# Sixteen rows of an output-weight load moved from SyncE to GpSimd, in pieces of 8191 elements and 1

## The chip, the cores and the metric

The kernel runs on one core of a Trainium2 chip. The metric is the device time of one execution in microseconds. Three runs of the kernel before gave 387.35, 387.57 and 392.26 us; their median is 387.57. The profiled execution took 387.31 us, of which 385.3 lie between the first and the last instruction.

## What is computed

A block for one decoded token in a batch of four: an adaptive layer norm, attention over a cache of 4096 positions with 32 query heads on 8 key/value heads, an output projection, a second adaptive layer norm, and a small mixer network. All is float32.

```
mod = (silu(c) @ w_mod).reshape(4, 6, 1, 512); sa, ca, ga, sb, cb, gb = mod[:, 0..5]
h = layernorm(x) * (1 + ca) + sa
q = (h @ wq), 32 heads of 128; k, v from the caches (4, 8, 4096, 128), each used by 4 query heads
o = softmax(q k^T / sqrt(128)) v
x = x + ga * (o @ wo)                       # wo is (32*128, 512)
h = layernorm(x) * (1 + cb) + sb
x = x + gb * (gelu(h * w1 + b1) @ w2 + b2)  # h is (4, 512), w1 and w2 have 1792 values
```

## The kernel before, in words

Nearly all bytes are the caches: 32 pairs of batch row and key/value head (index `i`, batch row `i // 8`, head `i % 8`), each with 2 MB of keys and 2 MB of values. With the query weights (8 MB), the output weights (8 MB) and the modulation weights (6 MB) the kernel reads 157.3 MB.

SyncE (SP) issues all loads. Its queue holds them in program order: the first modulation weights `wm01`, the small weights `sm` (two DMAs, rows 0 to 15 and rows 16 to 127, lines 50 and 51), `x`, two query-weight tiles, the keys of pairs 0 and 1 (`load_first`), and then one 4 MB tile per step that holds the keys of pair `i + 2` beside the values of pair `i` (`load_pair`, line 165). These 4 MB tiles, the query weights and some modulation weights share a ring of three buffers (`ring`, tag `kv`). So SP waits before an issue until TensorE has done with the buffer, and the DMA engines have two or so loads queued ahead meanwhile. The output weights have buffers of their own: `wo_p` (line 84) is four tiles of two heads each, 128 partitions by 4096 elements, and `load_wo` (line 171) loads one of them. They are loaded at lines 570 and 579 to 580: heads 0 and 1 before the loop, heads 2 and 3 in step 1, heads 4 and 5 in step 3, heads 6 and 7 in step 5.

Per pair, `scores` (line 217) multiplies the query with the keys into PSUM, VectorE reduces the row maximum, TensorE turns and spreads it, ScalarE takes the exponential, VectorE transposes the result in blocks, `values` (line 281) multiplies it with the values, and two steps later `project` (line 327) multiplies the head's output with that head's output weights `wo_t[h]`. A loop (lines 577 to 617) does pairs 0 to 23; the last eight follow an order written by hand (`PLAN`, line 626), in which the loads get shorter towards the end, the last ones being pieces of the values of pair 31 and then 1 MB of modulation weights. `Mixer` does the second half of the block for the first three batch rows between the attention steps; the last batch row's is the tail (`finish`, line 528).

GpSimd does small operations: constants, a few elementwise operations at the start up to the copy into `rows` (line 141), and then only the inverse square roots `root` (line 90) and `wr` (line 421) of the mixers.

Of the kernel before, what the change touches and what calls it, by code (L numbers as in the profile page):

```python
# [8 lines left out]
F32 = mybir.dt.float32  # L9
# [5 lines left out]
B, D, HQ, HKV, SK, DH, F = 4, 512, 32, 8, 4096, 128, 1792  # L15
REP = HQ // HKV
NF = F // 128
EPS = 1e-5
P = 128
NS = B * HKV  # L20
NSM = 3 * NF + 16 + 1


WIDE = {NS - 5: 24, NS - 4: 32}
NARROW = NS - 3


@with_exitstack
def adaln_decode(ctx: ExitStack, tc: tile.TileContext, small, x, wmod, wq, kk, kv, vv, wo, out):
    nc = tc.nc  # L30
    pad = ctx.enter_context(tc.tile_pool(name="pad", bufs=1))
    ring = ctx.enter_context(tc.tile_pool(name="ring", bufs=3))
    wos = ctx.enter_context(tc.tile_pool(name="wos", bufs=1))
# [12 lines left out]
    sm = cst.tile([P, NSM], F32, name="sm")  # L46
    xr = wk.tile([P, D], F32, name="xr", tag="yw", bufs=1)[0:B]
    wm01 = ring.tile([P, 2, 4, D], F32, name="wm01", tag="kv")
    nc.sync.dma_start(wm01, wmod[0])
    for lo, hi in ((0, 16), (16, P)):  # L50
        nc.sync.dma_start(sm[lo:hi], small[lo:hi])
    nc.sync.dma_start(xr, x)
    wqt = []
    for k in range(0, 4, 2):
# [26 lines left out]
    nc.gpsimd.memset(QT, 0.0)  # L81
    hT = cst.tile([P, 4, 32], F32, name="hT")
    nc.gpsimd.memset(hT, 0.0)
    wo_p = [wos.tile([P, 2, REP, D], F32, name=f"wo{h}") for h in range(0, HKV, 2)]
    wo_t = [wo_p[h // 2][:, h % 2] for h in range(HKV)]
    prep = cst.tile([P, 4, P], F32, name="prep")
    osb = cst.tile([P, B, P], F32, name="osb")
# [77 lines left out]
    def load_pair(i):  # L165
        t = slots()
        nc.sync.dma_start(t, kv[i])
        key(t[:, 0], i + 2)
        value(t[:, 1], i)

    def load_wo(h):
        nc.sync.dma_start(wo_p[h // 2], wo[h // 2])

    def load_wm24():
        w = ring.tile([P, 3, 4, D], F32, name="wm24", tag="kv")
# [133 lines left out]
    def pick(i):  # L309
        po = PV.pop(i)  # L310
        n, m = po.shape[-1] // DH, WIDE.get(i, 1)
        if i in OT:
# [255 lines left out]
    load_first()  # L568
    load_pair(0)
    load_wo(0)  # L570
    for i in range(2):
        for step in (scores, row_max, turn_max, col_max, spread_max, copy_max, expo):
            step(i)
# [3 lines left out]
    for i in range(NS - HKV):  # L577
        load_pair(i + 1)
        if i in (1, 3, 5):
            load_wo(i + 1)  # L580
# [155 lines left out]
```

## Time and profile before

| | us |
|---|---|
| median of three runs | 387.57 |
| profiled execution | 387.31 |
| its span, first to last instruction | 385.3 |
| TensorE busy in the span | 295.1 |
| VectorE busy | 195.9 |
| ScalarE busy | 111.5 |
| GpSimd busy | 8.5 |
| share of 16 DMA engines' span taken by SP's queue, q1 | 95.2% |

A core has 16 DMA engines. A load is cut into packets, each done by one engine; when an engine has done its part of a load it writes a completion, a packet of 4 bytes. The page gives packets by queue: q1 is SP's, q10 ScalarE's, and q8 and q14 fetch instructions. For a window of the trace the same table counts the packets that start in it, their bytes, and the time that they took as a share of 16 engines' time; from one kind of packet in a short window its duration follows.

### The profile page before, as it was taken

What the parts mean: (1) busy time and instruction counts of PE and PEld (TensorE: products, weight loads), DVE (VectorE), ACT (ScalarE), POOL (GpSimd) and SP (SyncE); (2) the same over time, 40 slices, a digit from 0 to 9 for tenths busy, and PEclk for the clock granted to TensorE, in tenths of its full rate; (3) what the DMA queues carried; (4) which work ended last, traced back from release to release, by engine and by line L of the source; (5) the groups of instructions that cost most, each with busy time, mean ns of one, the idle gap of its engine ahead of it and who ended that gap; (6) DMA issues with size and microseconds to landing.
All of it is one profiled execution on the core that took longest, in us unless ns stands there. A gap on an engine that the chain in (4) does not pass through costs nothing.

```text
span 385.3 us, 5577 instructions
## 1 busy us (share of the span) xinstructions
PE 295.1 (77%) x2376; PEld 118.0 (31%) x2376; DVE 195.9 (51%) x386; ACT 111.5 (29%) x141; POOL 8.5 (2%) x30
## 2 busy tenths in 40 slices
PE   0777594965856828799987869887788897889984
PEld 0122121311222302244432324342222453433753
DVE  0120441620443504546776544758665566878756
ACT  0001120121110111101577210124574105557266
POOL 1200000000000000000000000000000000000000
PEclk9969756985996979958999995999999999999999
DMA  8999999999999999999999999999999999999920
GB/s 331 432 435 435 413 456 435 405 454 429 412 441 432 427 432 435 430 435 434 432 435 435 430 433 434 432 430 432 427 435 432 430 432 428 422 428 427 416 92 3
DMA packets 7424, 157.68 MB, mean 409 GB/s; under 512 B 980, under 2 KB 1252, under 8 KB 1512
## 3 DMA queue, kind: packets, MB, share of 16 engines
q1 hardware_dynamic: 7392, 157.33, 95.2%
q8 instruction: 18, 0.29, 0.3%
q14 instruction: 6, 0.05, 0.0%
q10 hardware_dynamic: 8, 0.00, 0.0%
HBM read 157.32 MB, written 0.01 MB: 408 GB/s over the span
## 4 chain that ended last, share of the span: by engine, by line
DMA 55%; PE 32%; DVE 7%; ACT 3%; issue 1%; POOL 1%; SPq 0%; POOLq 0%; ACTq 0%; DVEq 0%
DMA kv<-in_kv 53%; PE s L222 8%; PE pv L282 8%; DVE p L258 3%; PE qs L129 3%; DVE m L227 3%; PE s L114 2%; PE pt L319 2%; DMA sm<-in_small 2%; PE pa L333 2%; PE pb L242 1%; ACT uu L538 1%; PE pve L294 1%; PE py L437 1%; PE pm L231 1%
## 5 line engine op out<-in xcount | busy, mean ns | idle before, releaser
L222 PE MATMUL s<-kv,QT 128*32 128x512 f32 x512 | 73.9, 697 | 44.1 <-DMA kv<-in_kv 42.9
L227 DVE TENSOR_REDUCE m<-s 128x1 f32<-128x1024 f32 x32 | 39.2, 1224 | 100.0 <-PE s L222 99.9
L252 ACT ACTIVATE p<-s,nm 128x1024 f32<-128x1024 f32 x32 | 35.6, 1114 | 181.9 <-DVE nm L247 181.8
L282 PE MATMUL pv<-kv,p 128*32 128x512 f32 x464 | 68.2, 655 | 0.5 <-DMA kv<-in_kv 0.5
L222 PEld LDWEIGHTS s<-kv,QT 128*32 128x32 f32 x512 | 15.8, 119 | 87.3 <-DMA kv<-in_kv 56.6
L319 PEld LDWEIGHTS pt<-g,po 128*128 128x128 f32 x236 | 30.6, 202 | 27.8 <-issue 21.3
L333 PE MATMUL pa<-wo,oT 128*32 128x512 f32 x240 | 33.7, 633 | 4.4 <-DVE oT L325 4.2
L319 PE MATMUL pt<-g,po 128*128 128x4 f32 (+2 forms) x236 | 33.4, 265 | 0.9 <-DVE po L305 0.8
L258 DVE STREAM_TRANSPOSE p<-p 128x1024 f32<-128x1024 f32 x25 | 30.9, 1235 | 0.0
L305 DVE COPY po<-pv 128x512 f32<-128x512 f32 x29 | 20.0, 689 | 15.2 <-PE pv L282 15.1
L236 DVE TENSOR_REDUCE mx<-pm 1x128 f32<-1x512 f32 x32 | 21.3, 669 | 1.0 <-PE pm L231 1.0
L426 DVE TENSOR_SCALAR u<-hb,wr,sm 128x512 f32<-128x512 f32 x40 | 19.9, 540 | 1.9 <-POOL wr L421 1.0
L482 ACT ACTIVATE u<-u 128x1024 f32<-128x1024 f32 x20 | 20.4, 1051 | 1.5 <-DVE u L426 1.4
L252 ACT ACT_TABLE_LOAD x11 | 14.1, 1283 | 19.4 <-DVE nm L247 19.3
L349 DVE TENSOR_TENSOR acc<-acc,pa 128x512 f32<-128x512 f32 x26 | 17.8, 686 | 2.8 <-PE pa L333 2.8
L242 PEld LDWEIGHTS pb<-neg,mx 1*128 1x128 f32 x64 | 10.2, 198 | 27.7 <-DVE mx L236 26.0
L114 PE MATMUL s<-wm,sT 128*4 128x512 f32 x16 | 9.2, 744 | 11.7 <-DVE sT L100 11.7
L482 ACT ACT_TABLE_LOAD x13 | 16.7, 1283 | 0.2
L282 PEld LDWEIGHTS pv<-kv,p 128*32 128x32 f32 x464 | 13.6, 146 | 6.8 <-issue 2.8
L231 PE MATMUL pm<-ident,m 128*1 128x128 f32 x32 | 9.1, 283 | 7.6 <-DVE m L227 3.5
L437 PE MATMUL py<-u,sm 128*32 128x512 f32 x80 | 14.5, 593 | 0.0
L242 PE MATMUL pb<-neg,mx 1*128 1x1 f32 x64 | 12.9, 268 | 2.1 <-DVE mx L236 2.1
(134 smaller groups left out, 213.5 us busy)
## 6 DMA issues: line engine op xcount, KB each, us to landing
kv<-in_kv SPq DMA_DIRECT2D x28, 4096.0 KB, 21.7
wq<-in_wq SPq DMA_DIRECT2D x2, 4096.0 KB, 15.8
wo<-in_wo SPq DMA_DIRECT2D x4, 2048.0 KB
kv<-in_kv SPq DMA_DIRECT2D x4, 2048.0 KB, 21.2
wm<-in_wmod SPq DMA_DIRECT2D x2, 2048.0 KB, 24.6
kv<-in_kk SPq DMA_DIRECT2D x1, 4096.0 KB
kv<-in_vv SPq DMA_DIRECT2D x3, 1024.0 KB
wm<-in_wmod SPq DMA_DIRECT2D x1, 1024.0 KB
```

The costliest lines, as they stand in the source:

```text
L222: mm(s[32 * c:32 * c + 32, n * 512:(n + 1) * 512], QT[:, b, h, :], KT[i][:, (n * 4 + c) * 512:(n * 4 + c + 1) * 512], start=True, stop=True)
L227: dv.tensor_reduce(M[i], S[i], axis=AX.X, op=OP.max)
L236: dv.tensor_reduce(mx, M[i].rearrange("o (c r) -> o r c", c=4).unsqueeze(1).to_broadcast([1, 4, 32, 4]), axis=AX.X, op=OP.max)
L242: mm(pb, M[i].rearrange("o c r -> o (c r)"), neg1, start=True, stop=True)
L252: nc.scalar.activation(p, S[i], AF.Exp, bias=M.pop(i), accum_out=l)
L258: dv.transpose(PL[i][0], PL[i][0])
L282: mm(PV[i][32 * q:32 * q + 32, :], pT[:, 128 * k:128 * k + 128:4], VT[i][:, 4 * k:4 * k + 4, :].rearrange("p j d -> p (j d)"), start=(k < ...
L305: dv.tensor_copy(PV[i], pv)
L319: mm(pt, po[:, c * DH:(c + 1) * DH], sel.unsqueeze(1).to_broadcast([P, m, REP]), start=(c == 0), stop=(c == n - 1))
L333: mm(pa[32 * g:32 * g + 32, :], oT[:, g:g + 1].to_broadcast([P, 32]), wo_t[h][:, g, :], start=True, stop=True)
L426: dv.tensor_scalar(u[:, e, :], hb, wr[:, j:j + 1], b1[:, j:j + 1], op0=OP.mult, op1=OP.add)
L482: nc.scalar.activation(u, u, AF.Gelu_apprx_tanh)
```

## The change

The output weights of heads 2 to 5 become one tile `wob` and one array in memory, laid out so that a partition's four heads, 8192 elements or 32 KB, lie in one piece. SP loads rows 0 to 111 of it in two DMAs (two heads each), where and when it loaded all 128 rows before. Rows 112 to 127 are loaded by GpSimd: for each row one DMA of 8191 elements and one of the last element, 32 in all. Heads 0, 1, 6 and 7 are loaded as before. The small weights are loaded in one DMA of 128 rows. The bytes are the same.

```diff
-    for lo, hi in ((0, 16), (16, P)):
-        nc.sync.dma_start(sm[lo:hi], small[lo:hi])
+    nc.sync.dma_start(sm, small)
...
-    wo_p = [wos.tile([P, 2, REP, D], F32, name=f"wo{h}") for h in range(0, HKV, 2)]
+    wo_b = wos.tile([P, 2, 2, REP, D], F32, name="wob")
+    wo_p = [wos.tile([P, 2, REP, D], F32, name=f"wo{h}") for h in (0, HKV - 2)]
+    wo_p[1:1] = [wo_b[:, 0], wo_b[:, 1]]
...
     def load_wo(h):
-        nc.sync.dma_start(wo_p[h // 2], wo[h // 2])
+        if h in (0, HKV - 2):
+            nc.sync.dma_start(wo_p[h // 2], wo[h // (HKV - 2)])
+        else:
+            nc.sync.dma_start(wo_p[h // 2][:LONG], wb[:LONG, h // 2 - 1])
+
+    def load_long():
+        n = 2 * SK
+        flat, src = wo_b.rearrange("p e h g n -> p (e h g n)"), wb.rearrange("p e h g n -> p (e h g n)")
+        for r in range(LONG, P):
+            for lo, hi in ((0, n - 1), (n - 1, n)):
+                nc.gpsimd.dma_start(flat[r:r + 1, lo:hi], src[r:r + 1, lo:hi])
...
     load_wo(0)
+    load_long()
```

`LONG` is 112. In the order of instructions it looks as follows. GpSimd before, around the copy into `rows`:

```order
L101 COPY sT_127<-sT 128x128 [waits DVE_49]
L109 TENSOR_SCALAR ve_139<-mv_137 4x1 [waits DVE_49]
L92 TENSOR_TENSOR yp<-ve_139,half 4x1 [waits Pool_49]
L141 COPY rows<-ident 4x32
L92 TENSOR_TENSOR ye<-mv,half 128x1 [waits DVE_49] x2
```

GpSimd now, from the same copy on (DMASW0 to 7 are eight semaphores that its DMAs use in turn):

```order
L143 COPY rows<-ident 4x32
L184 DMA wob<-in_wb 1x8191
L184 DMA wob<-in_wb 1x1
...
L184 DMA wob<-in_wb 1x8191 [waits DMASW0_49]
L184 DMA wob<-in_wb 1x1 [waits DMASW1_49]
...
L184 DMA wob<-in_wb 1x1 [waits DMASW7_49]
L94 TENSOR_TENSOR ye<-mv,half 128x1 [waits DVE_49] x2
```

The 32 issues stand between the copy and the first inverse square root of the mixers; from the ninth on each waits until the DMA eight places ahead has completed. SP before, from the loads ahead of the loop on (`wo_122` is heads 2 and 3):

```order
L172 DMA wo_121<-in_wo 128x4096
L167 DMA kv<-in_kv 128x8192 [waits DMAHW5_49,DMAHW1_49,PE_49]
L167 DMA kv<-in_kv 128x8192 [waits DMAHW6_49,DMAHW2_49,PE_49]
L172 DMA wo_122<-in_wo 128x4096 [waits DMAHW3_49]
L176 DMA wm_317<-in_wmod 128x4096 [waits DMAHW7_49,PE_49]
```

And now:

```order
L175 DMA wo_121<-in_wo 128x4096
L169 DMA kv<-in_kv 128x8192 [waits DMAHW4_49,PE_49]
L169 DMA kv<-in_kv 128x8192 [waits DMAHW5_49,DMAHW1_49,PE_49]
L177 DMA wob<-in_wb 112x4096 [waits DMAHW2_49]
L188 DMA wm_347<-in_wmod 128x4096 [waits DMAHW6_49,PE_49]
```

The load keeps its place and has 112 rows; SP's semaphores are one number lower, since one DMA less stands ahead of them. TensorE before, at the projection of head 2:

```order
L266 MATMUL pl<-g_115,l 128x4
L333 MATMUL pa<-wo_122,oT 32x512 [waits DMAHW3_49,DVE_49]
L333 MATMUL pa<-wo_122,oT 32x512 x3
L231 MATMUL pm<-ident,m 1x128 [waits DVE_49]
L282 MATMUL pv<-kv,p 32x512 x4
```

And now:

```order
L278 MATMUL pl<-g_114,l 128x4
L345 MATMUL pa<-wob,oT 32x512 [waits DMASW4_49,DMASW6_49,DMASW2_49,DMAHW2_49,DMASW0_49,DVE_49]
L345 MATMUL pa<-wob,oT 32x512 x3
L243 MATMUL pm<-ident,m 1x128 [waits DVE_49]
L294 MATMUL pv<-kv,p 32x512 x4
```

The projection of head 2 waits for GpSimd's long pieces beside SP's load; the order of TensorE's work is the same. In the same way the last matmul of head 5's projection waits for the pieces of one element.

More of the change, by code (lines that the diff above doesn't have):

```diff
@@ L21 @@
 NSM = 3 * NF + 16 + 1
+LONG = 112
 WIDE = {NS - 5: 24, NS - 4: 32}
@@ L28, in adaln_decode @@
 @with_exitstack
-def adaln_decode(ctx: ExitStack, tc: tile.TileContext, small, x, wmod, wq, kk, kv, vv, wo, out):
+def adaln_decode(ctx: ExitStack, tc: tile.TileContext, small, x, wmod, wq, kk, kv, vv, wo, wb, out):
     nc = tc.nc
@@ L717 @@
     v = a["A_v_cache"].reshape(NS, P, SK * DH // P)
+    w = a["A_wo"].reshape(HKV // 2, 2, REP, DH, D)
     arrays = {
@@ L725 @@
         "vv": con(v[NS - 2:]),
-        "wo": con(a["A_wo"].reshape(HKV // 2, 2, REP, DH, D).transpose(0, 3, 1, 2, 4)),
+        "wo": con(w[::3].transpose(0, 3, 1, 2, 4)),
+        "wb": con(w[1:3].transpose(3, 0, 1, 2, 4)),
     }
```

## The prediction, made before the result was known

> **What bounds the kernel now.** I read the page's shares and its chain first, then stretches of the span, then the DMA packets of short windows. From the page: the span, what the 16 DMA engines moved, the queues, and the chain's shares by engine.
>
> ```profile
> span 385.3 us, 5577 instructions
> GB/s 331 432 435 435 413 456 435 405 454 429 412 441 432 427 432 435 430 435 434 432 435 435 430 433 434 432 430 432 427 435 432 430 432 428 422 428 427 416 92 3
> ...
> q1 hardware_dynamic: 7392, 157.33, 95.2%
> q8 instruction: 18, 0.29, 0.3%
> q14 instruction: 6, 0.05, 0.0%
> ...
> DMA 55%; PE 32%; DVE 7%; ACT 3%; issue 1%; POOL 1%; SPq 0%; POOLq 0%; ACTq 0%; DVEq 0%
> ```
>
> From the second slice on the engines move about 432 GB/s until the last two slices. A table of four stretches says the same beside the compute engines (its last two columns are the DMA engines' busy share and GB/s):
>
> ```profile
> core 0: us, PE busy (x) PEld busy (x) DVE busy (x) ACT busy (x) POOL busy (x), PEclk, DMA share, GB/s
> 0.00:20.00 20.00, 8.32 (x15) 1.53 (x16) 1.56 (x5) 1.50 (x2) 3.82 (x19) 1.00 0.94 389
> 20.00:343.00 323.00, 251.52 (x1795) 95.59 (x1792) 164.19 (x309) 87.95 (x113) 3.95 (x9) 0.88 1.00 431
> 343.00:367.00 24.00, 23.39 (x348) 13.04 (x348) 18.95 (x42) 10.75 (x14) 0.00 (x0) 1.00 1.00 420
> 367.00:386.00 19.00, 11.91 (x228) 7.82 (x220) 11.24 (x31) 11.29 (x14) 0.76 (x2) 0.97 0.07 30
> ```
>
> From 20 to 367 us the DMA engines are busy all the time. TensorE has 71 us to spare up to 343, then 0.61 us in the stretch to 367, then 19 us of tail follow. So the end is the end of the stream plus the tail. A load has landed when its slowest engine is done, so what counts is the latest of 16 engines. A completion is a 4-byte packet, one from each engine that a load used; they are the packets under 512 B in these windows. First the end of the load that lands near 18 us, then that of the load near 342 us, cut in three:
>
> ```profile
> DMA packets 32, 0.52 MB, mean 477 GB/s; under 512 B 16, under 2 KB 16, under 8 KB 16
> ```
> ```profile
> DMA packets 59, 0.82 MB, mean 431 GB/s; under 512 B 9, under 2 KB 9, under 8 KB 9
> ```
> ```profile
> DMA packets 21, 0.34 MB, mean 430 GB/s; under 512 B 0, under 2 KB 0, under 8 KB 0
> ```
> ```profile
> DMA packets 26, 0.31 MB, mean 445 GB/s; under 512 B 7, under 2 KB 7, under 8 KB 7
> ```
>
> The first window is 17.1 to 18.2: all 16 engines finish within 1.1 us. The others are 339.2 to 341.1, to 341.9 and to 342.6: nine engines finish in the first 1.9 us, none in the next 0.8, seven in the last 0.7. So seven engines run about 3 us behind the first, and they set the pace. What else those engines carry is the instruction fetches of q8 and q14, 24 packets. One of them, in the window 98.4 to 99.4:
>
> ```profile
> q1 hardware_dynamic: 14, 0.46, 109.6%
> q8 instruction: 1, 0.02, 5.5%
> ```
>
> 5.5% of 16 engines in 1.0 us is 0.88 us of one engine.
>
> **Prices of a packet.** Windows with packets of one size: 20 to 26 us (32 KB), 4.8 to 6.8 (16 KB), and 7.264 to 7.270 (one completion):
>
> ```profile
> q1 hardware_dynamic: 77, 2.52, 97.3%
> ```
> ```profile
> q1 hardware_dynamic: 50, 0.82, 95.5%
> ```
> ```profile
> q1 hardware_dynamic: 1, 0.00, 9.4%
> ```
>
> 0.973 x 16 x 6.0 / 77 = 1.21 us for 32 KB; 0.955 x 16 x 2.0 / 50 = 0.61 us for 16 KB; 0.094 x 16 x 6 ns = 9 ns for a completion.
>
> **The change, part by part.** *Two loads of 112 rows.* How rows go to engines is seen where the small loads end, 7.25 to 8.4:
>
> ```profile
> DMA packets 201, 0.58 MB, mean 504 GB/s; under 512 B 180, under 2 KB 180, under 8 KB 184
> ```
>
> 180 packets are the 128 rows of the small weights and 52 completions; 52 = 16 (modulation weights) + 16 (the 16 rows) + 16 (the 112 rows) + 4 (x, whose 4 rows are the four 2 KB packets). So 112 rows go to 16 engines, seven each, and an engine loses one 16 KB packet in each of two loads: 2 x 0.61 = -1.22 us on every engine. That is the lower end. The upper end is not shown, since the 112 small rows are too short to tell; the packets of such a load could be held up by each other (second rival). I take -1.22, which the nearest row, the 112-row load with seven rows an engine, gives.
>
> *Sixteen long pieces.* 8191 elements are 32764 B, by the rows of 32 KB above one packet of 1.21 us, together 16 x 1.21 = 19.4 us of engine time. Spread evenly this is +1.21 an engine, and nothing is gained or lost. An engine that is missed has 0, one that gets two 2.43; all on one engine would be 19.4 (a rival). The 32 pieces alternate long and short, so if engines are taken in turn, every second engine gets two long ones and the others none. I take 2.43 for the latest engine: with half of the engines drawn, one of the seven late ones is almost surely among them. Net +1.21.
>
> *Completions.* 32 more DMAs: at least one completion each, at most one on all 16 engines, 0.0 to 32 x 9 ns = 0.3 us on an engine. I take 0.1, since x had one for each engine that it used. If each held its engine as the fetch above did (0.88 us against 0.61 for its 16 KB on q1, 0.27 too much), 32 x 0.27 = 8.6 us: the upper end, which I do not take, as a completion carries 4 bytes. The Trainium skill, DMA: Bandwidth & Descriptors, "Why a DMA increments its semaphore by 16 and not by 1", says that a DMA issued by GpSimd completes on all 16 engines whatever its shape, and that one with no common divisor goes to a single engine that a cursor picks in turn; no run here shows either. By it the sum would be 0.2 higher, and there would be no pile on one engine (third rival).
>
> *Small weights in one load.* SP issues one DMA less, and 16 completions go, 9 ns on each engine. SP has nothing to do then until 20.94, and no engine of the stream waits for it:
>
> ```profile
> 1.18 0.87 SPq L51 DMA_DIRECT2D sm<-in_small  x2
> ...
> 20.94 0.33 SPq L161 DMA_DIRECT2D kv<-in_kk  x1
> ```
>
> The weights land at most 0.1 us earlier, and what hides it is the full stream. I count 0; if the cover were gone it would be a gain of 0.1.
>
> *GpSimd's queue and the new wait.* 32 issues stand between two of its instructions, and TensorE's projection of head 2 now waits for them:
>
> ```profile
> 13.32 0.20 POOL L141 COPY rows<-ident 4x32 f32<-4x32 f32 x1
> 173.56 0.57 POOL L92 TENSOR_TENSOR ye<-mv,half 128x1 f32<-128x1 f32 x1 [160.05 <-DVE mv L383]
> ```
> ```profile
> 99.61 1.06 PE L333 MATMUL pa<-wo,oT 128*32 128x512 f32 x8 [0.21 <-DVE oT L325]
> ```
>
> GpSimd is idle for 160 us after its copy, and the pieces have 99.6 - 13.5 = 86 us. Eight are in flight at a time; at SP's 0.44 us an issue the 32 take 14 us, at the 21.7 us in which a large load of SP lands (the page's row below) four rounds take 87. Only then does TensorE stall, by about 1 us, with everything behind the projection, and it has those 71 us to make it up. I count 0.
>
> ```profile
> kv<-in_kv SPq DMA_DIRECT2D x28, 4096.0 KB, 21.7
> ```
>
> *How it reaches the end.* TensorE is idle for 0.61 us between 343 and 367, and what it waited for from the loads between 326 and 368 is
>
> ```profile
> PE s L222 <- DMA kv<-in_kv: 2.4, 3, 1.2
> ```
>
> A later stream moves all that follows by as much; an earlier one is worth at most these 2.4 us.
>
> **Sum.** -1.22 + 2.43 + 0.1 = +1.3 us. The profiled execution took 387.31 us (385.3 of span and 2.0 around it), 0.3 below the median of 387.57. 387.3 + 1.3 = 388.6; against the median 388.9. I say 388.8.
>
> **Rivals.** *Not slower: the late engines are spared.* If the long pieces fall just on engines that are ahead, the seven late ones keep only the -1.22. For: the nine early ones have 0.8 us and more in hand, and the alternation of long and short looks as if it picked engines. Against: a set of every second engine has to miss all seven. The early ones then come 1.2 later, to about 0.3 us before the old end, so 0.3 to 1.1 us are won: 386.2 to 387.0. It decides where no late engine gets two pieces.
>
> *Slower: rows that go to other engines than usual hold each other up.* In loads of 128 rows each engine moves eight rows of its own, undisturbed, at 27 GB/s. If writes to the same rows of SBUF share one engine's rate, then seven rows an engine, shifted against the usual eight, meet the packets of neighbours that are in another load. Each of 14 packets then goes at half speed, +14 x 0.61 = 8.6 us, and each engine is also met by as many, up to 8.6 more; the long pieces add 1.2 (met once) to 4.9 (rows 112 to 127 are four engines' rows, four pieces each). With the -1.2: +7.4 to +20.9, or 395 to 408, middle 402. For: no load of the stream has another shape than 128 rows, so no row excludes it. Against: the packets of the 112 small rows show no stretch. It decides if more than about half of the packets meet another. The Trainium skill speaks for it: SBUF — State Buffer, "Door 1: The DMA port swizzle", gives each group of eight partitions one port with about one engine's rate; that 16 engines of 27 GB/s make 432 here agrees with it, but with a limit of the engines as well.
>
> *Slower: piled up or surcharged.* All long pieces on one engine, as x's four rows went to four engines and a one-row load might always go to the first: 19.4 - 1.2 = 18.2, less up to 3 us if that engine is ahead: 402 to 405. Or 32 completions on every engine at 0.27: 396.
>
> **Chances.** The forecast (387.8 to 390.6) 0.34; late engines spared 0.18; rows that meet 0.32; piled up or surcharged 0.10; rows that meet only now and then (391 to 395) 0.04; more than 2% faster 0.02. 2% is 7.8 us, about what a measurement of this kernel can tell from no change: below 379.8 is faster, above 395.3 slower. Within: 0.34 + 0.18 + 0.04 = 0.56; slower 0.32 + 0.10 = 0.42; faster 0.02. The range leaves out the best of the spared case and the worst third of the meeting one: 386.0 to 404.0. The forecast's own range is 387.8 to 390.6.
>
> **What would show it.** Right: 32 KB packets stay at 1.21 us in all windows, the late completions of the load near 342 us come 1 us later, and the loads land as before up to there. Spared: the seven late completions come earlier. Meeting rows: packets of 16 or 32 KB far over 0.61 and 1.21 us between 14 and 115 us, GB/s under 400 in slices of that part, and all later loads late by the same. Surcharge: the same between 14 and 60 us, with 512 and not 32 new completions. Wrong in any case: a wait of TensorE at the projection of head 2 that costs the end.

## The result and the profile after

The changed kernel takes 432.09 us (median of four runs, 431.37 to 432.37); beside it on the same chip the kernel before took 387.46. The ratio is 1.1145 (95% interval 1.1111 to 1.1179), 44.6 us more. The prediction said 388.8 and at most 404. The profiled execution has a span of 430.1 us; before it was 385.3. Executions that were disturbed are left out of the ratios here and below, so a ratio can differ a little from the quotient of two medians.

These are the page's lines of the changed kernel that answer to those shown of before: the span, GB/s in 40 slices of now 10.75 us, the queues (q0 is GpSimd's), and the chain's shares.

```profile
span 430.1 us, 5614 instructions
...
GB/s 345 427 418 421 414 422 341 255 142 34 360 422 253 388 407 443 282 424 364 421 416 399 420 436 434 433 431 436 343 439 428 419 427 434 431 422 433 409 89 3
...
q1 hardware_dynamic: 7344, 156.81, 89.4%
q0 software_dynamic: 1024, 0.53, 0.6%
...
DMA 54%; PE 28%; another core or an unknown queue 7%; DVE 6%; ACT 2%; issue 1%; POOL 1%; SPq 0%; POOLq 0%; DVEq 0%; ACTq 0%
```

The stream falls to 34 GB/s in the tenth slice (97 to 107 us) and dips again later. The table of stretches of the changed kernel gives its size (the last three columns are the granted TensorE clock, the DMA engines' busy share and GB/s); the stretch from 388 on is the one that before began at 343.

```profile
core 0: us, PE busy (x) PEld busy (x) DVE busy (x) ACT busy (x) POOL busy (x), PEclk, DMA share, GB/s
0.00:20.00 20.00, 8.74 (x16) 1.49 (x16) 1.56 (x5) 1.50 (x2) 8.13 (x27) 1.00 0.93 379
20.00:64.00 44.00, 20.55 (x129) 6.53 (x132) 7.67 (x12) 4.07 (x10) 7.22 (x14) 0.75 1.01 421
64.00:108.00 44.00, 18.58 (x98) 5.84 (x94) 8.34 (x14) 2.41 (x4) 5.24 (x11) 0.59 0.65 193
108.00:150.00 42.00, 23.89 (x158) 6.66 (x154) 9.75 (x18) 4.76 (x9) 0.00 (x0) 0.69 0.99 358
150.00:388.00 238.00, 192.45 (x1420) 76.31 (x1412) 138.60 (x266) 76.39 (x90) 3.95 (x9) 0.92 0.97 413
388.00:412.00 24.00, 23.42 (x346) 13.03 (x348) 18.67 (x42) 11.17 (x14) 0.00 (x0) 1.00 0.95 397
```

And the same stretches of the kernel before, up to 150 us:

```profile
0.00:20.00 20.00, 8.32 (x15) 1.53 (x16) 1.56 (x5) 1.50 (x2) 3.82 (x19) 1.00 0.94 389
20.00:64.00 44.00, 28.64 (x172) 9.01 (x173) 11.52 (x18) 5.27 (x12) 0.00 (x0) 0.73 1.00 431
64.00:108.00 44.00, 33.70 (x237) 10.97 (x233) 15.99 (x28) 5.96 (x11) 0.00 (x0) 0.81 1.00 428
108.00:150.00 42.00, 25.19 (x176) 8.37 (x168) 15.66 (x28) 3.61 (x6) 0.00 (x0) 0.84 1.01 436
```

In bytes: by 150 us the changed kernel has moved 379 x 20 + 421 x 44 + 193 x 44 + 358 x 42 = 49.6 MB, the kernel before 63.9 MB in the same way. The missing 14.3 MB are 33 us at 431 GB/s. From 150 to 388 it moves 413 and not 431: 238 x 18 = 4.3 MB, another 10 us. Those 43 us are nearly all of it; the tail after the stream is as before. So the loss is in the stream, three quarters of it before 150 us.

Two things happen there. First, one engine is left alone. In the window 97 to 107 of the changed kernel the queues show

```profile
q1 hardware_dynamic: 13, 0.25, 5.7%
q0 software_dynamic: 40, 0.07, 1.7%
```

One engine is 1/16 = 6.25%. These 7.4% are hardly more than one engine's time, and fifteen engines have nothing to do. The completions of a load tell why; these are the 16 completions of three loads, in us (the trace's own events):

```
load near 28 us:  27.36 27.51 27.55 27.61 27.67 27.71 27.84 27.85 27.86 27.99 28.00 28.01 28.13 28.17 30.41 34.82
load near 62 us:  61.34 61.47 61.50 61.58 61.63 61.67 61.79 61.80 61.99 62.13 62.15 62.24 62.33 67.06 68.53 95.23
load near 72 us:  71.10 71.30 71.32 71.60 71.89 71.89 71.91 72.18 72.25 72.47 73.03 73.13 73.41 81.14 84.08 107.18
```

One engine is 7 us behind the first at 28 us, 34 at 62 and 36 at 72; two others are late by less. A load has landed when that engine is done; with all three buffers waiting for it, SP cannot issue. One 4 MB load of the changed kernel, issued at 40.6, and the one in its place before, issued at 34.1 (the last number is us from issue to landing):

```profile
kv<-in_kv SPq DMA_DIRECT2D x1, 4096.0 KB, 54.6
```
```profile
kv<-in_kv SPq DMA_DIRECT2D x1, 4096.0 KB, 28.9
```

The chain of the changed kernel names no load at the place where TensorE waits for the second of those three (start and length in us):

```profile
71.38 23.85 another core or an unknown queue
```

It ends at 95.23, the very time of that load's last completion. What TensorE waited for from these loads (us in total, times, longest), of the changed kernel and before:

```profile
PE s L234 <- DMA kv<-in_kv: 66.2, 21, 23.9
```
```profile
PE s L222 <- DMA kv<-in_kv: 42.9, 21, 7.4
```

Second, packets are longer. In the window 20 to 26 the queues of the changed kernel show

```profile
q1 hardware_dynamic: 77, 2.52, 99.0%
q0 software_dynamic: 77, 0.03, 2.8%
```

One long piece and 76 packets of 9 ns took 0.028 x 96 = 2.69 us, so the piece took 2.0, not 1.21; SP's 32 KB packets stay near their old 1.21 (0.990 x 96 / 77 = 1.23). The trace's single packets say more: while the piece ran, from 23.45 to 25.46, just one packet of SP's was much longer, 2.15 us; the packet that starts where the piece ends took 1.55 and the one that starts where that longer packet ends 1.57; the other 74 took 1.21 or 1.22. So this piece held up one packet beside it and, by a quarter or so, the two behind, and not all engines. From 72 to 78, where the first load of 112 rows goes through:

```profile
q1 hardware_dynamic: 83, 1.39, 99.3%
```

1.39 MB are 85 times 16 KB, in 0.993 x 96 = 95.3 us of engine time: 1.12 us for each 16 KB. Before, the window 75 to 80 is full of 16 KB packets:

```profile
q1 hardware_dynamic: 148, 2.16, 101.0%
```

132 packets of 16 KB and 16 completions in 1.01 x 80 = 80.8 us: 0.61 each.

GpSimd's part looks harmless: eight issues in a row, then each waits for a DMA before it, the last issue being at 97.21; TensorE's projection of head 2, now at 142.80 us, still waits for VectorE and not for the pieces.

```profile
13.05 4.35 POOL L184 DMA_DIRECT2D wob<-in_wb  x8
21.01 0.52 POOL L184 DMA_DIRECT2D wob<-in_wb  x1 [3.62 <-DMA wob<-in_wb]
...
97.21 0.52 POOL L184 DMA_DIRECT2D wob<-in_wb  x1 [1.38 <-DMA wob<-in_wb]
```
```profile
142.80 1.06 PE L345 MATMUL pa<-wob,oT 128*32 128x512 f32 x8 [0.18 <-DVE oT L337]
```

### The profile page after: what moved, and what is told of

Same layout as the page of the kernel before. It is cut to its first block, busy times and chain, and to the rows that moved or that the text cites. A ratio compares the mean times of both kernels' runs of the same rounds, so it can differ in the third digit from the quotient of the medians.

```text
span 430.1 us, 5614 instructions
## 1 busy us (share of the span) xinstructions
PE 299.5 (70%) x2376; PEld 117.7 (27%) x2376; DVE 195.8 (46%) x386; ACT 111.5 (26%) x141; POOL 25.3 (6%) x62
## 3 DMA queue, kind: packets, MB, share of 16 engines
q0 software_dynamic: 1024, 0.53, 0.6%
## 4 chain that ended last, share of the span: by engine, by line
DMA 54%; PE 28%; another core or an unknown queue 7%; DVE 6%; ACT 2%; issue 1%; POOL 1%; SPq 0%; POOLq 0%; DVEq 0%; ACTq 0%
DMA kv<-in_kv 50%; PE s L234 7%; PE pv L294 7%; DVE m L239 2%; DMA kv<-in_vv 2%; PE s L116 2%; PE pa L345 2%; DVE p L270 2%; PE pt L331 2%; DMA sm<-in_small 2%; PE pm L218 1%; ACT uu L550 1%; PE pb L254 1%; PE pve L306 1%; PE qs L131 1%
## 5 line engine op out<-in xcount | busy, mean ns | idle before, releaser
L234 PE MATMUL s<-kv,QT 128*32 128x512 f32 x512 | 76.6, 718 | 72.3 <-DMA kv<-in_kv 66.2
L94 POOL TENSOR_TENSOR ye<-mv,half 128x1 f32<-128x1 f32 x7 | 3.9, 553 | 316.4 <-DVE mv L395 316.4
L184 POOL DMA_DIRECT2D wob<-in_wb x32 | 16.8, 527 | 67.9 <-DMA wob<-in_wb 67.9
L345 PE MATMUL pa<-wob,oT 128*32 128x512 f32 x128 | 18.1, 630 | 2.3 <-DVE oT L337 2.3
L361 DVE TENSOR_TENSOR acc<-acc,pa 128x512 f32<-128x512 f32 x26 | 17.8, 686 | 3.9 <-PE pa L345 3.7
L345 PE MATMUL pa<-wo,oT 128*32 128x512 f32 x112 | 16.7, 668 | 1.8 <-DVE oT L337 1.7
L116 PE MATMUL s<-wm,sT 128*4 128x512 f32 x16 | 8.9, 722 | 11.3 <-DVE sT L102 11.3
L449 PE MATMUL py<-u,sm 128*32 128x512 f32 x80 | 15.4, 617 | 0.0
```

Source lines behind the costliest of these rows:

```text
L234: mm(s[32 * c:32 * c + 32, n * 512:(n + 1) * 512], QT[:, b, h, :], KT[i][:, (n * 4 + c) * 512:(n * 4 + c + 1) * 512], start=True, stop=True)
L345: mm(pa[32 * g:32 * g + 32, :], oT[:, g:g + 1].to_broadcast([P, 32]), wo_t[h][:, g, :], start=True, stop=True)
L361: dv.tensor_add(ACC[b], ACC[b], pa)
```

## The experiments

My theory after the result was that two of the rivals hold at once: *pile* (all sixteen long pieces go to one engine) and *meeting rows* (the loads of 112 rows give rows to other engines than usual, and packets hold each other up). Against them stood *in turn* (engines taken in turn by alternating long and short pieces, so that half of the engines are hit) and *surcharge* (32 more DMAs cost time on every engine whatever they carry). All experiments compute the same output; where a kernel loads something twice or into a tile that nothing reads, it is said. All were timed against the kernel before on the same chip, whose median was 387.47 to 387.52.

**Order of the pieces** (against the changed kernel): all long pieces first, then the single elements.

```diff
-        for r in range(LONG, P):
-            for lo, hi in ((0, n - 1), (n - 1, n)):
+        for lo, hi in ((0, n - 1), (n - 1, n)):
+            for r in range(LONG, P):
```

> The changed kernel with GpSimd's 32 DMAs in another order: first the 16 long pieces, then the 16 pieces of one element. Theory A (the DMA engines are taken in turn, one step per DMA, and the alternation of long and short put the long pieces on few engines): the long pieces now go to 16 engines, one each, no engine falls behind by more than 3 us for them, and the time drops from 432 to 395 to 405 us. Theory B (a piece of one row always goes to the same engine, as the four rows of x went to four engines): all 16 long pieces stay on one engine, one of 16 completions of each load comes up to 36 us after the others as in the changed kernel, and the time stays at 428 to 434 us.

428.05 us, ratio 1.1019 (1.0947 to 1.1092). If engines were taken in turn, sixteen long pieces in a row would have been spread over all. They were not; the 16 completions of SP's load near 62 us (the trace's own events, in us):

```
61.70 62.05 62.12 62.13 62.27 62.31 62.35 62.35 62.38 62.41 62.47 62.49 65.85 67.17 68.73 100.63
```

One engine is 39 us behind the first, as in the changed kernel. *In turn* falls, and the pile does not come from the alternation. The time is 4 us below the changed kernel's, a little more than the two intervals cover; the reason was not looked for.

**Rows split, GpSimd left out:** SP loads rows 112 to 127 in a DMA of 16 rows behind each load of 112 rows.

```diff
             nc.sync.dma_start(wo_p[h // 2][:LONG], wb[:LONG, h // 2 - 1])
+            nc.sync.dma_start(wo_p[h // 2][LONG:], wb[LONG:, h // 2 - 1])
...
-    load_long()
```

> GpSimd issues nothing; SP loads rows 112 to 127 as a second DMA of 16 rows behind each of the two loads of 112 rows. Theory of the piled engine (the whole loss is one engine that has all long pieces): no engine is piled, 386 to 389 us. Theory of meeting rows (loads of 112 rows go at half speed since seven rows an engine are not the engine's usual rows): packets of 16 KB take about 1.1 instead of 0.61 us around these loads, 395 to 405 us.

399.88 us, ratio 1.0292 (1.0226 to 1.0358): +12.4 by the medians, with no piece of GpSimd's. Its span and GB/s (slices of 9.9 us), and its queue from 75 to 80:

```profile
span 397.1 us, 5577 instructions
...
GB/s 324 426 446 444 404 444 426 277 394 423 393 237 422 414 432 432 451 432 424 426 428 442 441 426 423 424 449 434 429 421 436 441 432 428 420 429 420 415 70 2
```
```profile
q1 hardware_dynamic: 95, 1.10, 101.7%
```

There are just two dips, 277 and 237, at the two loads that are split. 1.10 MB are 67 packets of 16 KB, the other 28 are completions: (1.017 x 80 - 0.3) / 67 = 1.21 us a packet, twice the 0.61 of before, with the engines fully busy. The 32 KB packets of neighbouring loads that pass at the same time are stretched too: in the window 115 to 120, behind the second split load, 31 of them took 1.89 us on average.

**Rows split, sixteen rows by GpSimd in one DMA** (SP's loads of 112 rows stay).

```diff
-        for r in range(LONG, P):
-            for lo, hi in ((0, n - 1), (n - 1, n)):
-                nc.gpsimd.dma_start(flat[r:r + 1, lo:hi], src[r:r + 1, lo:hi])
+        nc.gpsimd.dma_start(flat[LONG:], src[LONG:])
```

> GpSimd loads rows 112 to 127 in one DMA of 16 rows of 8192 elements instead of 32 DMAs of one row; SP's loads of 112 rows stay. Piled engine: the 16 rows go to 16 engines, 32 KB each, and the time is 386 to 390 us. Meeting rows: the loads of 112 rows still go at half speed, and the 16 rows slow the four engines whose rows they are: 396 to 408 us. Surcharge (each of GpSimd's 32 DMAs costs every engine something): little of it is left with one DMA, 387 to 390 us.

401.79 us, ratio 1.0323 (1.0243 to 1.0403), about the same as with SP. GpSimd's queue in the window 17 to 23 has 32 packets, 16 of data and 16 completions:

```profile
q0 software_dynamic: 32, 0.52, 64.4%
```

The 16 packets of data all start between 17.1 and 17.8 us and are under way at once: 16 rows in one DMA go to 16 engines, and then nothing is left of the pile. About 30 us of the change hang on its pieces being single rows. Each packet took 0.644 x 96 / 16 = 3.9 us, though, and not 1.21: sixteen engines wrote into 16 neighbouring rows at once, which fits *meeting rows*.

**Small weights alone:** the kernel before with its one load.

```diff
-    for lo, hi in ((0, 16), (16, P)):
-        nc.sync.dma_start(sm[lo:hi], small[lo:hi])
+    nc.sync.dma_start(sm, small)
```

> The kernel before with the small weights in one load and nothing else of the change. All theories: within 0.5 us of before, 387 to 388 us; if the completions of the first load matter, 0.1 us less.

387.29 us, ratio 0.9984 (0.9956 to 1.0012). Nothing, as predicted.

**Pieces alone, late:** SP loads all 128 rows; GpSimd's 32 pieces load rows 112 to 127 once more, in step 7 of the loop.

```diff
-            nc.sync.dma_start(wo_p[h // 2][:LONG], wb[:LONG, h // 2 - 1])
+            nc.sync.dma_start(wo_p[h // 2], wb[:, h // 2 - 1])
...
-    load_long()
...
+        if i == 7:
+            load_long()
```

> SP loads all 128 rows of the output weights of heads 2 to 5, as in the kernel before; GpSimd's 32 DMAs stay but come only after step 7 of the loop, and load rows 112 to 127 a second time with the same values (0.5 MB more than the changed kernel). So there are no loads of 112 rows, only the pieces. Piled engine: one completion of each load falls behind the other 15 by up to 30 to 37 us, and the time is 416 to 426 us. If the pile mattered only together with the loads of 112 rows: 388 to 395 us.

426.22 us, ratio 1.1021 (1.0987 to 1.1056): the pieces are dear without any split load. But the place has a price of its own, as the next kernel showed.

**The same place, pieces of one element** (the same edit, and the long piece cut to one element):

```diff
-            for lo, hi in ((0, n - 1), (n - 1, n)):
+            for lo, hi in ((n - 2, n - 1), (n - 1, n)):
```

> Like the kernel with the pieces loaded again after step 7, but both pieces of each row are one element long, so that GpSimd's 32 DMAs, their completions and waits are all there and hardly a byte is moved. Piled engine: nothing is left of the loss, 387 to 389 us. Surcharge (each DMA of GpSimd makes each engine change between two queues and costs it some 0.3 us): 32 x 0.3 us more, 395 to 400 us.

404.41 us, ratio 1.0431 (1.0416 to 1.0447): 17 us for 32 elements, which neither theory had expected. The stretches of that kernel, then its GpSimd, then its TensorE:

```profile
core 0: us, PE busy (x) PEld busy (x) DVE busy (x) ACT busy (x) POOL busy (x), PEclk, DMA share, GB/s
...
192.00:203.00 11.00, 8.80 (x49) 4.76 (x53) 5.65 (x12) 1.78 (x3) 1.35 (x4) 0.62 0.00 0
```
```profile
191.48 0.52 POOL L184 DMA_DIRECT2D wob<-in_wb  x1 [2.61 <-DMA wob<-in_wb]
192.02 0.59 POOL L94 TENSOR_TENSOR ye<-mv,half 128x1 f32<-128x1 f32 x1
```
```profile
194.19 1.01 PE L331 MATMUL pt<-g,po 128*128 128x4 f32 x4 [19.84 <-DVE po L317]
```

The inverse square root of the first mixer stands behind the 32 issues in GpSimd's queue, each of which waits some 2 us for the DMA eight ahead; only after the last of them does it run. VectorE waits 20.75 us for it, and only then TensorE, 19.84 us idle, goes on. So the cost is that of a blocked queue and says nothing on the pieces. The kernel before it holds the same cost, and is no price of the pile.

**Pieces of one element at the change's own place**, where no GpSimd instruction is due for long; they go to a tile that nothing reads, SP loads all 128 rows.

```diff
-            nc.sync.dma_start(wo_p[h // 2][:LONG], wb[:LONG, h // 2 - 1])
+            nc.sync.dma_start(wo_p[h // 2], wb[:, h // 2 - 1])
...
+        scrap = cst.tile([P, 2], F32, name="scrap")
         for r in range(LONG, P):
-            for lo, hi in ((0, n - 1), (n - 1, n)):
-                nc.gpsimd.dma_start(flat[r:r + 1, lo:hi], src[r:r + 1, lo:hi])
+            for e in range(2):
+                nc.gpsimd.dma_start(scrap[r:r + 1, e:e + 1], src[r:r + 1, n - 2 + e:n - 1 + e])
```

> SP loads all 128 rows. GpSimd's 32 DMAs stand where the change has them, after the copy into rows and 150 us before its next work, but each loads one element into a small tile that nothing reads. In the run with the tiny pieces behind step 7 the DMA engines stood idle at about 192 to 203 us while GpSimd's inverse square root stood behind its DMAs. Theory of the blocked queue: here nothing of GpSimd is waited for in that time, and the time is 387 to 388.5 us. Surcharge (each of the 32 DMAs makes each engine change between two queues, 0.3 us each): 395 to 400 us.

387.81 us, ratio 1.0018 (0.9995 to 1.0042). *Surcharge* falls, though there are far more packets than I had counted:

```profile
q0 software_dynamic: 1024, 0.00, 0.1%
```

1024 packets for 32 DMAs: 32 for each, although it moves one element; dealt out evenly that is two on each of 16 engines. They take 0.1% of the engines' time.

**Pieces alone at the change's own place:** SP loads all 128 rows of everything; 32 DMAs of one row and 4093 elements load rows 96 to 127 of heads 6 and 7, which SP's load brings again later. These are as many bytes as the sixteen long pieces.

```diff
-            nc.sync.dma_start(wo_p[h // 2][:LONG], wb[:LONG, h // 2 - 1])
+            nc.sync.dma_start(wo_p[h // 2], wb[:, h // 2 - 1])
...
+        flat, src = (t.rearrange("p h g n -> p (h g n)") for t in (wo_p[3], wo[1]))
-        for r in range(LONG, P):
-            for lo, hi in ((0, n - 1), (n - 1, n)):
-                nc.gpsimd.dma_start(flat[r:r + 1, lo:hi], src[r:r + 1, lo:hi])
+        for r in range(96, P):
+            nc.gpsimd.dma_start(flat[r:r + 1, :4093], src[r:r + 1, :4093])
```

> SP loads all 128 rows everywhere, so no load has 112 rows. GpSimd's 32 DMAs stand where the change has them, each of one row and 4093 elements (16 KB): rows 96 to 127 of the tile of heads 6 and 7, which SP's load of the same 128 rows overwrites later with the same values. That is the changed kernel's number of DMAs and its bytes by GpSimd, 0.5 MB more in all. Piled engine: one of 16 completions falls behind by 30 us or more, 412 to 425 us; with 12.4 us for the loads of 112 rows it should give about the changed kernel's 44.6 us, so 419. If the pieces were spread over the engines: 388 to 392 us.

417.53 us, ratio 1.0782 (1.0766 to 1.0798): +30.0 from the pieces alone. Its page, and its queues from 88 to 96:

```profile
span 416.8 us, 5622 instructions
...
GB/s 340 421 432 404 423 412 409 410 75 231 382 443 367 407 447 417 443 253 418 313 393 383 428 439 425 433 434 431 439 423 434 432 431 431 433 420 425 416 84 3
```
```profile
q1 hardware_dynamic: 7, 0.20, 5.7%
q0 software_dynamic: 39, 0.05, 1.6%
```

The picture of the changed kernel without its split rows: 5.7 + 1.6 = 7.3%, again one engine at work and fifteen idle, and this with 32 pieces of 16 KB from 32 different rows. The trace gives the 32 pieces 23.1 us in all, and while the stream is full the 32 KB packet that starts where a piece ends takes 1.5 us and not 1.21. Other engines fall a few us behind as well; the completions of three loads:

```
load near 28 us:  27.41 27.65 27.66 27.69 27.76 27.77 27.85 27.86 27.87 27.94 28.03 28.06 28.14 28.15 30.15 33.14
load near 37 us:  37.04 37.29 37.32 37.34 37.37 37.40 37.49 37.52 37.60 37.66 37.71 37.76 37.77 39.27 39.77 48.18
load near 62 us:  61.84 61.94 61.97 61.98 62.01 62.09 62.23 62.29 62.34 62.40 63.95 63.96 64.46 64.50 64.57 86.49
```

By 28 us the pieces of rows 96 to 99 have started, and one engine beside the piled one is 2 to 3 us behind the first; by 37 us those up to row 102, and two are; by 62 us those up to row 110, and five are, of which one is 1.9 us behind in the kernel before as well. In the changed kernel, whose pieces begin at row 112, it is one near 28 us (rows 112 and 113 have started) and two near 62 us (up to row 118). That is about one more engine for each four rows, so what a piece holds up depends on its rows. This is read from the traces; no kernel was made to test it.

More is lost later, when TensorE has a backlog. The stretches 200 to 215 of this kernel and 165 to 176 of the changed one:

```profile
200.00:215.00 15.00, 14.63 (x92) 6.17 (x88) 7.82 (x18) 2.41 (x4) 1.12 (x2) 0.72 0.80 324
```
```profile
165.00:176.00 11.00, 11.00 (x57) 4.04 (x53) 4.04 (x7) 1.21 (x2) 0.00 (x0) 0.52 0.75 323
```

TensorE has hardly a pause, at a granted clock of 0.72 and 0.52, and a fifth to a quarter of the DMA time is idle. From 150 on the changed kernel's DMA share is 0.97, so 0.03 x 238 = 7 us are given up there; before it was 1.00.

**Rows split in all four output-weight loads** (by SP, 112 + 16 rows, no GpSimd).

```diff
-            nc.sync.dma_start(wo_p[h // 2], wo[h // (HKV - 2)])
+            nc.sync.dma_start(wo_p[h // 2][:LONG], wo[h // (HKV - 2)][:LONG])
+            nc.sync.dma_start(wo_p[h // 2][LONG:], wo[h // (HKV - 2)][LONG:])
...
+            nc.sync.dma_start(wo_p[h // 2][LONG:], wb[LONG:, h // 2 - 1])
...
-    load_long()
```

> All four loads of output weights in 112 and 16 rows by SP, not only the two of heads 2 to 5. Meeting rows: the loss of two such loads, 12.4 us, doubles, 410 to 415 us; the later of them, which the stream reaches with engines further apart, may cost a little more. If only the first such load disturbed the engines and the rest followed from it: 400 to 404 us.

422.18 us, ratio 1.0785 (1.0697 to 1.0872): by the ratio +30 (27 to 34), where two such loads cost 11.3 by theirs. The four runs lie far apart, from 414.97 to 424.55. The direction is that of *meeting rows*, the size is missed, and why four cost more than twice two is not settled.

**Columns split, by SP:** each of the two loads as 3584 and 512 columns of all 128 rows.

```diff
-            nc.sync.dma_start(wo_p[h // 2][:LONG], wb[:LONG, h // 2 - 1])
+            t, w = (z.rearrange("p h g n -> p (h g n)") for z in (wo_p[h // 2], wb[:, h // 2 - 1]))
+            for lo, hi in ((0, 3584), (3584, 4096)):
+                nc.sync.dma_start(t[:, lo:hi], w[:, lo:hi])
...
-    load_long()
```

> As many DMAs of SP and as many bytes as with 112 and 16 rows, but cut across: each of the two loads goes as 128 rows of 3584 elements and 128 rows of 512 elements, and GpSimd issues nothing. Meeting rows: each engine keeps its eight usual rows, no packet is held up, 387 to 388.5 us. If instead the second DMA of a load, or a new layout of the array in memory, costs the time: 395 to 402 us, as with rows.

387.45 us, ratio 1.0000 (0.9990 to 1.0009). As many DMAs and as many bytes apart as in the rows' split, and no cost at all: neither the further DMAs nor the joint array in memory cost anything, the rows do.

**Columns split, by GpSimd:** SP loads 3584 columns of 128 rows, GpSimd the other 512 in one DMA for each load.

```diff
-            nc.sync.dma_start(wo_p[h // 2][:LONG], wb[:LONG, h // 2 - 1])
+            t, w = (z.rearrange("p h g n -> p (h g n)") for z in (wo_p[h // 2], wb[:, h // 2 - 1]))
+            nc.sync.dma_start(t[:, :3584], w[:, :3584])
...
-        for r in range(LONG, P):
-            for lo, hi in ((0, n - 1), (n - 1, n)):
-                nc.gpsimd.dma_start(flat[r:r + 1, lo:hi], src[r:r + 1, lo:hi])
+        for e in range(2):
+            t, w = (z.rearrange("p h g n -> p (h g n)") for z in (wo_b[:, e], wb[:, e]))
+            nc.gpsimd.dma_start(t[:, 3584:], w[:, 3584:])
```

> The same eighth of the bytes goes from SP to GpSimd, but cut across: of each of the two loads SP takes 128 rows of 3584 elements, GpSimd 128 rows of 512 elements in one DMA at the place of the change. All engines keep their rows and have the same bytes. Piled engine and meeting rows: 387 to 388 us, neither is there. If GpSimd as the issuer cost something of itself: 390 us or more.

387.42 us, ratio 0.9998 (0.9989 to 1.0007). The window 75 to 80 of this kernel, where its first split load passes:

```profile
q1 hardware_dynamic: 154, 2.18, 102.6%
```

Full rate. As many bytes go over to GpSimd as in the change; that GpSimd issues them costs nothing, if each engine keeps its rows.

**Pieces of two rows:** eight DMAs of two rows and 8191 elements, and the last elements of 16 rows in one.

```diff
-        for r in range(LONG, P):
-            for lo, hi in ((0, n - 1), (n - 1, n)):
-                nc.gpsimd.dma_start(flat[r:r + 1, lo:hi], src[r:r + 1, lo:hi])
+        for r in range(LONG, P, 2):
+            nc.gpsimd.dma_start(flat[r:r + 2, :n - 1], src[r:r + 2, :n - 1])
+        nc.gpsimd.dma_start(flat[LONG:, n - 1:], src[LONG:, n - 1:])
```

> The changed kernel, but GpSimd's long pieces go as eight DMAs of two rows of 8191 elements, and the 16 last elements as one DMA of 16 rows. Piled engine (a DMA of k rows uses the same first k engines each time): two engines get eight pieces each, half the pile, so about half of what the pile costs beside the loads of 112 rows: 432 less 15 is 414 to 420 us. If the pieces go to two engines in turn: 400 to 406 us, as with one DMA of 16 rows.

424.97 us, ratio 1.0915 (1.0846 to 1.0984), later than the 414 to 420 I expected of a pile on two engines. The completions of one of SP's loads in the trace, in us:

```
39.35 39.45 39.47 39.55 39.56 39.64 39.67 39.70 39.87 39.89 39.93 40.00 44.22 44.40 61.71 63.72
```

Now two engines are late, by 22 to 24 us; a two-row DMA takes two engines, and each of the eight the same two. Each has half of the long pieces, but a piece now took 2.0 to 3.1 us in the trace. That the two pieces, of neighbouring rows and at the same time, hold each other up would fit; it was not tried apart. It does not explain that most of SP's packets are longer here too. Its queue from 18 to 24:

```profile
q1 hardware_dynamic: 58, 1.84, 86.8%
```

0.868 x 96 / 58 = 1.44 us for each 32 KB, where the changed kernel had 1.23 from 20 to 26. Why is open.

## Why the prediction was wrong, step by step

*"Two loads of 112 rows", taken at -1.22: wrong.* Measured without GpSimd's pieces, as loads of 112 and 16 rows, the split is +12.4 (the second experiment; by its ratio 11.3 us); no run has the 112 rows without the other 16. The step counted bytes for each engine and took the rate as given. It is the second rival that holds, with a price inside its range: without the pieces its own terms give 8.6 - 1.2 = 7.4 to 17.2 - 1.2 = 16.0. (The lower end that it states, 7.4 with the pieces, leaves out the 1.2 that they were to add at least.) The packets of the split loads go at half speed. Column splits of the same size cost nothing, so it is the change of rows among engines and not the number or size of DMAs. That engines which write to the same rows hold each other up is what the pieces show as well: about one more late engine for each four rows. That they meet at a shared port is argued from this, not shown. The Trainium skill, SBUF — State Buffer, "Door 1: The DMA port swizzle", gives each group of eight partitions one port. Two engines that write there at once would have to share it, and the runs agree with that: 1.21 us against 0.61.

*"Sixteen long pieces", taken at 2.43 on the latest engine: wrong, and the larger error.* The step chose "engines are taken in turn" where no row spoke for it. All sixteen went to one engine: 44.6 in the whole, +30.0 by the pieces alone. The third rival named the pile, and then mis-sized it in two ways. It took 1.21 us a piece, 19.4 in all; the trace has 1.8 to 2.1 while the other engines run (the first twelve), 1.21 while they stand still (the next three), 2.35 for the last, 29.5 us in all. And it took the end as late as that engine, which is not the whole: the others starve, TensorE gets its work in bunches, and 7 us of DMA time are lost again after 150 us. The cursor that takes engines in turn, for which the prediction cited the Trainium skill (DMA: Bandwidth & Descriptors, "Why a DMA increments its semaphore by 16 and not by 1"), is not what these runs show: sixteen one-row DMAs in a row, and in another kernel 32 of them, went to one and the same engine, and eight two-row DMAs to the same two. How the hardware picks them was not found.

*The sum of both:* 12.4 + 30.0 = 42.4 of 44.6. The 2.2 left lie within the interval of the first term (its ratio is known to 0.7%, or 2.6 us). The sum is rough, though: the kernel of the first term has DMAs of 16 rows that the change has not, and that of the second moves 0.5 MB more than the change, in pieces that took 23.1 us and not 29.5. The two causes make up nearly all of it; a third one of a few us is not excluded. I gave the two as separate cases, 0.32 and 0.10, and no chance to both at once, though one does not exclude the other; that left 44 us outside every case.

*"Completions", 0.1, and no surcharge: right,* though for packets that I had undercounted: 1024, which make 0.3 us by the medians (387.81 against 387.52) and nothing outside the interval. That GpSimd's DMAs complete on all 16 engines, as the Trainium skill says in the section just named, agrees with the 1024.

*"Small weights in one load", 0: right* (387.29). *"GpSimd's queue and the new wait", 0: right* in the number, with some luck: the projection of head 2 waited 0.18 us, for VectorE. The issues took from 13.05 to 97.7 us, 85 us, close to the four rounds of 87 that I had as the bound. But the last long piece, issued at 95.31, landed 20.6 us later, at 115.9, and so 16 us behind the 99.6 us at which the projection stood before. It was not waited for because the late stream had moved the projection to 142.80. Where the same issues stand ahead of a mixer they cost 17 us.

*"How it reaches the end": right as to the end, wrong before it.* The tail is unchanged, but "TensorE has 71 us to spare" did not hold in places: with its work bunched and a granted clock of 0.52 it had none between 165 and 176 us.

## What to carry to other kernels

In a stream that fills the DMA engines, cut a load along its columns and keep all 128 rows in each part: a cut along rows halved the packets' rate, a cut along columns was free. Don't move rows one at a time: single-row DMAs can all land on one engine, a load is as late as its latest engine, and a ring of buffers lets the other fifteen starve; count what each engine gets from the completions of a load, not from the bytes. Before DMA issues are put into an engine's queue, look at what stands behind them, since an issue that waits for an earlier DMA holds back everything after it.

## What the runs showed of the hardware

- A one-row DMA from GpSimd goes to a single engine, and 16 or 32 of them in a row went to the same one; two-row DMAs all went to the same two; a DMA of 16 rows went to 16.
- In a full stream a one-row piece of 32 KB took 2.0 us and not 1.21, and one of SP's packets beside it 2.15. With pieces of rows 96 to 110 four or five engines fell 2 to 3 us behind, with pieces of rows 112 to 118 two, by 6 to 7 us: about one for each four rows.
- Each of GpSimd's 32 DMAs made 32 packets, also for a single element; 1024 of them cost nothing that can be measured (387.81 against 387.52 us).
- A packet of 16 KB took 1.21 us and not 0.61 in loads whose rows were dealt out otherwise than those of the loads around them, with the engines counted as fully busy. A busy share of 1.00 is no proof of full rate: here it was 1.02 at 220 GB/s, where the kernel before had 1.01 at 433.
- With eight DMAs in flight in a full stream, GpSimd mostly got one issue away in 2.4 us even where a DMA moved a single element, as these lines of its timeline show (pieces of one element at the change's own place):

```profile
23.41 0.52 POOL L185 DMA_DIRECT2D scrap<-in_wb  x1 [1.91 <-DMA scrap<-in_wb]
25.83 0.52 POOL L185 DMA_DIRECT2D scrap<-in_wb  x1 [1.90 <-DMA scrap<-in_wb]
28.26 0.52 POOL L185 DMA_DIRECT2D scrap<-in_wb  x1 [1.91 <-DMA scrap<-in_wb]
```
